# A two-part fp32 kernel on one core: the constant of a softmax sum added on another engine, an integer shift routed through PSUM, and a hand-planned list with new due steps

## The chip, the core and the metric

The kernel runs on one core of a Trainium2 chip. The metric is device time in microseconds (us) of one execution. The core has five engines that matter here: TensorE (PE, matmuls; PEld are its weight loads), VectorE (DVE), ScalarE (ACT), GpSimd (POOL) and SyncE (SP, which only issues DMAs). Each works through its own list of instructions in order and waits on semaphores for the others.

## The reference

An attention block and then a gated feed-forward block. The attention is computed per batch b (8) and head (8), with 512 tokens x and 32 state rows, head size 64:

```python
scores = scale * x @ state.T;  scores -= scores.max(-1)
a = exp(scores);   a /= a.sum(-1) + 1e-9;   xread = a @ state
scores2 = scale * state @ x.T; scores2 -= scores2.max(-1)
a2 = exp(scores2); a2 /= a2.sum(-1) + 1e-9; sread = a2 @ x
y = concat([xread, sread], axis=2)      # -> 4352 tokens x 512
h = y @ w_in        # 512 x 2048
g = h * cos(h)
out = g @ w_out     # 2048 x 512
```

x and state are float32; w_in and w_out arrive as float64 and are brought to float32 bits on the chip. "The constant" of the title is the 1e-9.

## The kernel before

**Data and stages.** Heads' reads are folded into the first feed-forward product: for each batch and each 512 columns of w_in, `products` (L484) multiplies the states with w_in, giving weight columns sw_all; a tile of h (128 hidden columns by 512 tokens) is then sw_all times the softmax weights aT_all. Each h tile goes through the gate: `gate` (L594, ACT: rounding to an integer, with bias 0.25), `gate2` (L601, DVE: subtract), `gate3` (L604, ACT: sine), `gate4` (L608, DVE: multiply, into g_all). The products of g with w_out collect in the two PSUM banks o (acc). From the third batch on, both products are done by a seven-product scheme on half-size blocks: `sw_sums` (L549, GpSimd) makes its weight sums, `seven_part` (L565, PE) its products, `seven_sum` (L583, DVE) the sums into h that the next part has to wait for, and `Product` does the same for w_out, with blocks fetched from DRAM into a ring and sums made on GpSimd.

**PSUM.** `at` has two banks (scores, transposes, reads), `o` two, and h_pairs[1] two, called side banks (L180, L181): in the first pair they hold the results of `products` until ACT or DVE has copied them to sw_all. Two more single banks hold the h tiles of the first pair, so the tile two places on waits for `gate4` of this one.

**An attention.** Class `Attention`: `max1` and `max2` reduce the scores, `spread1` spreads a row of 16 values per partition over a tile, `shift` subtracts, `exps` (L393, ACT) does both exponentials, the second one with its sums accumulated on the way into i12, `sums1` (L412, DVE) the sums of the first. `inverse` (L401) adds 1e-9 to the 34 sums per partition (32 of the first softmax, 2 of the second; the tile is named i_all in the profile) and takes the reciprocal, both on DVE; `spread1` and `norm1` (L422) then normalize. In the first pair `inverse1`, `inverse2` and `inverse12` call it, four times in all; later `spread2` (L415) calls it once for each of attentions 3 to 7.

**Conversion.** `fetch` (L226) loads a raw block of float64 pairs into slots of g_all, and `convert` (L238) makes float32 of it in five steps: "1" and "2" on ACT (magnitude of the high words, top bits of the low words), "b" on DVE (a shift left by 3, in place on SBUF), "c" on DVE (sign bit XORed in; one instruction with two tensors), "d" on GpSimd (an integer add). Blocks 0 to 3 have 512 elements per partition, blocks 4 to 17 have 1024. A block's slot comes free for the next raw block once "2" and "c" have read it.

**The order.** Two mechanisms set it. The first pair of batches (32 tiles, steps 0 to 31) is a hand-written list of tasks (`first_pair_tasks`, L1162). Each task has an engine, an assumed cost, the names of what it reads and writes, a due step, and a flag for those that need the port shared with GpSimd. `link` (L1559) derives the dependences and turns a due step into a time (22 + PACE x step), `first_pair` (L1595) then picks tasks engine by engine: among those that can start within NEAR of the earliest, the one due first. ARRIVED (L995) is when the first seven raw blocks are taken to be in; CONV and CONV_DUE (L1555, L1556) order the conversions of blocks 4 to 17; the raw load of a block is due three steps ahead of its conversion. Idle PE stretches at the start are filled with matmuls on zeros (`warm`). Instructions issued in this way carry line L44 in the profile.

Everything later is recorded on a tape (`taping[0]` is true) in program order, and `in_order` (L1821) reorders it by the assumed costs of `cost_of` (L1743) and by due times derived back from PE's place. `works_of` (L1773) marks the DVE operations taken to share the port with GpSimd. These instructions carry L1868. Nothing of either plan is decided at run time: each engine gets a fixed list.

Of the kernel before, what the change touches and what calls it, by code (L numbers as in the profile page):

```python
# [11 lines left out]
I32 = mybir.dt.int32  # L12
U32 = mybir.dt.uint32
ALU = mybir.AluOpType
# [8 lines left out]
def kernel(  # L23
# [32 lines left out]
    nc = Lanes  # L56
# [36 lines left out]
    TEMPS = 4  # L93
# [144 lines left out]
    def convert(i, p):  # L238
        if not f64:
            return  # L240
        raw, dst = raws[i], loads[i][0]
        bits = dst.bitcast(I32)
        m, w = dst.shape[1:]
        c0 = m * w if i in (2, 3) else 0
        e = low[i % 2][:, c0:c0 + m * w].rearrange("p (m f) -> p m f", m=m)
        e = e.bitcast(I32)
        if p == "1":
            nc.scalar.activation(dst, raw.bitcast(F32)[:, :, :, 1],
                                 func=ACTF.Abs, scale=2.0 ** -112)
        elif p == "2":  # L250
            nc.scalar.activation(e, raw.bitcast(U32)[:, :, :, 0],
                                 func=ACTF.Copy, scale=2.0 ** -29)
        elif p == "b":
            nc.vector.tensor_scalar(bits, bits, 3, None,
                                    op0=ALU.logical_shift_left)
        elif p == "c":
            nc.vector.scalar_tensor_tensor(out=bits, in0=raw[:, :, :, 1],
                                           scalar=-2 ** 31, in1=bits,
                                           op0=ALU.bitwise_and,
                                           op1=ALU.bitwise_xor)  # L260
        else:
            nc.gpsimd.tensor_tensor(bits, bits, e, op=ALU.add)
# [10 lines left out]
    class Attention:  # L273
# [126 lines left out]

        def inverse(self, v):  # L401
            w = v.rearrange("p (a b) -> p b a", b=2)
            nc.vector.tensor_scalar(w, w, 1e-9, None, op0=ALU.add)
            nc.vector.reciprocal(v, v)

        def inverse1(self):
# [585 lines left out]
                             stop=True)  # L992

    WARM, START_PE = 8, 19.7
    ARRIVED = (10.0, 11.3, 12.7, 14.0, 16.6, 19.3, 22.0)  # L995

    single_pool = singles.__enter__()
    for i in range(7 if f64 else 5):
# [163 lines left out]
    def first_pair_tasks():  # L1162
# [10 lines left out]
        def dve(n):  # L1173
            return .06 + n * .00108
# [23 lines left out]
        def conversion(i, due):  # L1198
            n = 512 if i < 4 else 1024
            raw, w, e = raw_of(i), weight_of(i), low_of(i)  # L1200
            if i > (6 if f64 else 4):
                add("sp", .4, lambda: fetch(i), "", raw, due - 3)
            for p, engine, cost, r, wr, sh in (
                    ("1", "act", act(n) + .05, raw, w, False),
                    ("2", "act", act(n) + .05, raw, e, False),
                    ("b", "dve", n * .0007 + .03, w, w, True),
                    ("c", "dve", dve(n), raw + " " + w, w, True),
                    ("d", "pool", pool(n), e + " " + w, w, False)):
                add(engine, cost, lambda p=p: convert(i, p), r, wr, due,
                    sh)  # L1210

        def attention(b, k):
# [26 lines left out]
            for j in range(2 if b == 0 else 0):  # L1239
                add("act", act(512) + .03,  # L1240
                    lambda j=j: a.exp1(slice(j, j + 1)), f"z{z}{j}",
                    f"z{z}{j}", k + 4)
            m2 = k + 6 if b == 0 else k + 4
            if b == 0:
                for j in range(2):
                    add("dve", .62, lambda j=j: a.sums1((j,)), f"z{z}{j}",
# [81 lines left out]
        def tile_(t, k):  # L1328
            n = t.b * NF + t.f
            h, z, c = n % 2, t.b % 2, t.f // 4 % 2  # L1330
            g = names(quads_of[t.row][t.i // QT], t.i % QT)
            add("pe", 1.72, lambda: hidden(t),
                f"sw{c}{t.f % 4 // 2}0 sw{c}{t.f % 4 // 2}1 z{z}0 z{z}1",
                f"h{h} H", k)
            add("act", act(512) - .04, lambda: gate(t), f"h{h}", f"q{h}")
            add("dve", dve(512) - .02, lambda: gate2(t), f"h{h} q{h}", f"q{h}")
            add("act", .63 if n else 1.91, lambda: gate3(t), f"q{h} T",
                f"q{h}")
            add("dve", dve(512) - .02, lambda: gate4(t), f"h{h} q{h}", g,
                k + 2)  # L1340

        def inner(which, m, q, temps, to, k, raw=True):
            for i in range(4):
# [144 lines left out]
            at_step[max(0, int(due) - 1)].append(  # L1488
                lambda i=i, due=due: conversion(i, due))
        for step, what in (  # L1490
                (1, lambda: attention_late(0, 0)),
                (3, lambda: products(0, 1, 2.5)),
                (3, lambda: add("pe", .4, lambda: states(1, side_banks[0]),
                                "held0", "sd00 sd01", 8.5)),
                (3, lambda: add("act", .53,
                                lambda: states_kept(1, side_banks[0]),
                                "sd00 sd01", "stT1", 5.5)),
                (5, lambda: attention(1, 4)),
                (7, lambda: products(0, 2, 4.5)),
                (11, lambda: products(0, 3, 11.5)),  # L1500
                (13, lambda: products(1, 0, 16)),
                (13, lambda: attention_late(1, 18)),
                (13, lambda: inner(0, a11, 5, temps[0], names(TEMPS), 14.5)),
                (15, lambda: sends(2, a22, 8, 17)),
                (15, lambda: sums_of(SQ, A21, A22, add_, 16, "pool")),
                (16, lambda: products(1, 1, 18.5)),
                (16, lambda: inner(3, matrix(SQ), SQ, temps[1], E, 17)),
                (17, lambda: sums_of(A22, SQ, A11, sub_, 16, "pool")),
                (17, lambda: attention(2, 19)),
                (18, lambda: sums_of(A21, A11, A21, sub_, 20, "dve")),  # L1510
                (20, lambda: products(1, 2, 23)),
                (20, lambda: inner(5, matrix(A21), A21, temps[0],
                                   names(TEMPS), 20)),
                (20, lambda: sends(1, a12, 6, 22)),
                (21, lambda: inner(4, matrix(A22), A22, temps[1], E, 22)),
                (23, lambda: sums_of(SQ, A12, A22, sub_, 23, "dve")),
                (24, lambda: inner(6, matrix(SQ), SQ, temps[0], names(TEMPS),
                                   25)),
                (24, lambda: products(1, 3, 31)),
                (25, lambda: attention_late(2, 25)),  # L1520
                (24, lambda: [add("sp", .4, lambda n=n: fetch_block(n), "B3",
                                  f"ring{n}", 27) for n in range(NB - 1)])):
            at_step[step].append(what)
        t32, t34 = all_tiles[PERIOD], all_tiles[PERIOD + 2]
        for step, what in (
                (26, lambda: outer(0, 2, 0, 0, 26, "dve")),
                (27, lambda: outer(0, 2, 0, 1, 27, "dve")),
                (28, lambda: tokens_of_next(32)),
                (28, lambda: products(2, 0, 28)),
                (28, lambda: p5_tasks(30.5)),  # L1530
                (29, lambda: weight_columns(t32, 30.5)),
                (29, lambda: add("dve", .7, lambda: halves(2, 0), "z00 z01",
                                 "E0", 30, True)),
                (29, lambda: add("dve", .7, lambda: halves(2, 1),
                                 "z00 z01 E0", "E1", 30, True)),
                (30, lambda: seven_tasks(t32, 29.5)),
                (31, lambda: weight_columns(t34, 32)),
                (32, lambda: outer(2, 3, 2, 0, 32, "dve")),
                (32, lambda: p3_sums(32))):
# [203 lines left out]
    def cost_of(engine, op, kw, aps):  # L1743
# [29 lines left out]
    def works_of(tape):  # L1773
        works, last, at_ = [], {}, 0.0
        wrote, read = {}, defaultdict(list)
        for engine, op, f, args, kw, n in tape:
# [167 lines left out]
```

## Time and profile before

| what | value |
|---|---|
| time, median of 3 runs | 739.65 us (737.28 to 739.89) |
| the profiled execution's own time | 744.15 us |
| its span, first to last instruction | 742.4 us |
| mean granted PE clock | 0.98 of full speed |
| instructions | 10,727 |
| first pair (L44), PE's last matmul ends | about 161 us |
| matmuls in the first pair's stretch 0 to 161 us, PE busy | 146.2 us |
| from 161 us on, PE busy | 558.5 of 581.4 us |

How to read it. The profile comes from one execution, which took 744.15 us by itself; its span leaves out 1.75 us around it. Busy time of PE is wall time with a matmul in flight, at whatever clock was granted. A row of the timeline gives start, duration, engine, line, operation, output<-inputs, and in square brackets how long the engine stood idle before it and what released it. For DVE and GpSimd the duration of a row includes any time that the instruction, already started, was held up. In the rows by tile, three numbers with slashes are shortest, median and longest duration in nanoseconds. In the list of waits, the numbers are the sum, the count and the longest.

### The profile page before, as it was taken

The page shows a single profiled execution, that of the slowest core. Times are in us where ns is not written, and L with a number is a line of the kernel's source. Part 1 is how long each engine was busy: PE and PEld are TensorE (multiplying, and loading weights), DVE is VectorE, ACT ScalarE, POOL GpSimd, SP SyncE. Part 2 cuts the span into 40 slices and gives each one's busy share as a digit, 9 for nine tenths or more (in the row PEclk, how much of TensorE's full clock was granted, in tenths as well). Part 3 has the DMA queues.
Part 4 walks back from the last instruction along what each step waited for, and adds up shares of the span by engine and source line. Part 5 has one row for each costly group of instructions (what it writes and reads, how often), then busy time and mean ns, then how long its engine had stood idle before and what let it go on. Part 6 is the DMA issues. An engine that isn't in the chain of part 4 may idle for free.

```text
span 742.4 us, 10727 instructions
## 1 busy us (share of the span) xinstructions
PE 704.7 (95%) x3628; PEld 525.4 (71%) x3628; DVE 524.7 (71%) x703; ACT 347.6 (47%) x586; POOL 536.9 (72%) x524
## 2 busy tenths in 40 slices
PE   8898799899959999999869999999999999999997
PEld 3343344477847878787757878887778888888886
DVE  4999769887897687788877667777875466725530
ACT  5788866654623446344624456343634443211110
POOL 1565779578974998988947975798978848896600
PEclk9999999999979999999979999999999999999999
DMA  9964689655517854783326734772356245455851
GB/s 299 291 223 154 214 229 326 137 144 139 143 42 141 218 131 119 154 182 82 97 54 133 183 79 103 154 177 79 107 135 178 86 100 130 113 195 175 220 104 29
DMA packets 204022, 111.34 MB, mean 150 GB/s; under 512 B 149888, under 2 KB 166784, under 8 KB 203968
## 3 DMA queue, kind: packets, MB, share of 16 engines
q1 hardware_dynamic: 202880, 110.14, 57.1%
q8 instruction: 29, 0.48, 0.3%
q10 hardware_dynamic: 960, 0.39, 0.2%
q14 instruction: 25, 0.20, 0.1%
q0 software_dynamic: 128, 0.13, 0.1%
HBM read 87.03 MB, written 23.59 MB: 149 GB/s over the span
## 4 chain that ended last, share of the span: by engine, by line
PE 79%; DVE 10%; ACT 5%; DMA 3%; issue 2%; SPq 1%; ACTq 0%; DVEq 0%
PE o L1868 39%; PE h L1868 22%; PE at L1868 8%; PE h L44 6%; PE o L44 4%; DVE i_all L1868 3%; DMA g_all<-in_moe_w_out_dram 2%; DVE g_all L44 2%; ACT q_all L44 1%; DVE q_all L44 1%; PE at L44 1%; ACT L44 1%; DVE q_all L1868 1%; DMA g_all<-blocks_kept 1%; DVE aS_all L1868 1%
## 5 line engine op out<-in xcount | busy, mean ns | idle before, releaser
L1868 POOL TENSOR_TENSOR g_all<-g_all 128x512 f32<-128x512 f32 x250 | 323.3, 1321 | 31.8 <-PE o L1868 21.3
L1868 PE MATMUL o<-g_all 128*128 128x256 f32 x1448 | 341.9, 382 | 0.0
L1868 PEld LDWEIGHTS o<-g_all 128*128 128x128 f32 x1448 | 273.7, 191 | 46.9 <-issue 5.6
L1868 ACT ACTIVATE q_all<-h 128x1024 int32<-128x1024 f32 (+1 forms) x56 | 54.0, 965 | 123.6 <-PE h L1868 122.1
L1868 DVE TENSOR_TENSOR q_all<-q_all,h 128x1024 f32<-128x1024 int32 (+1 forms) x56 | 63.9, 1141 | 48.1 <-ACT q_all L1868 47.8
L1868 DVE TENSOR_TENSOR g_all<-h,q_all 128x1024 f32<-128x1024 f32 (+1 forms) x56 | 64.0, 1142 | 25.7 <-ACT q_all L1868 23.6
L1868 PE MATMUL h<-aS_all,sw_all 128*128 128x256 f32 x188 | 57.4, 387 | 18.4 <-DVE h L1868 18.4
L1868 ACT ACTIVATE q_all<-q_all,halfpi 128x1024 f32<-128x1024 f32 (+1 forms) x56 | 61.1, 1091 | 27.5 <-DVE q_all L1868 27.2
L44 PE MATMUL h<-aT_all,sw_all 128*128 128x512 f32 (+1 forms) x132 | 65.5, 624 | 6.2 <-DVE g_all L44 6.2
L1868 DVE TENSOR_TENSOR h<-h,sums_all 128x256 f32<-128x256 f32 x94 | 40.2, 428 | 39.0 <-PE h L1868 33.7
L1868 DVE TENSOR_TENSOR g_all<-g_all 128x1024 f32<-128x1024 f32 (+1 forms) x68 | 67.5, 1036 | 0.1
L1868 POOL TENSOR_TENSOR swS_all<-sw_all 128x128 f32<-128x128 f32 x46 | 23.6, 514 | 49.3 <-ACT sw_all L1868 48.9
L1868 PE MATMUL h<-aS_all,swS_all 128*128 128x256 f32 x188 | 59.0, 396 | 0.0
L1868 PE MATMUL h<-aT_all,sw_all 128*128 128x256 f32 x188 | 56.6, 383 | 0.0
L1868 PEld LDWEIGHTS h<-aS_all,sw_all 128*128 128x128 f32 x188 | 35.6, 192 | 25.0 <-DVE h L1868 10.1
L44 PEld LDWEIGHTS h<-aT_all,sw_all 128*128 128x128 f32 x132 | 24.5, 197 | 37.5 <-issue 20.5
L1868 PEld LDWEIGHTS h<-aS_all,swS_all 128*128 128x128 f32 x188 | 34.0, 191 | 21.3 <-POOL g_all L1868 10.1
L44 POOL TENSOR_TENSOR g_all<-g_all 128x512 f32<-128x512 f32 x30 | 40.4, 1363 | 7.4 <-DVE g_all L44 4.8
L44 PE MATMUL o<-g_all 128*128 128x512 f32 (+1 forms) x112 | 43.7, 520 | 0.0
L44 POOL TENSOR_TENSOR w_in<-w_in,aS_all 128x1024 int32<-128x1024 int32 (+1 forms) x10 | 21.4, 2155 | 27.8 <-DVE w_in L44 22.5
L1868 POOL TENSOR_TENSOR held<-held 128x512 f32<-128x512 f32 x16 | 21.2, 1329 | 26.3 <-DVE held L1868 22.2
L1868 PEld LDWEIGHTS h<-aT_all,sw_all 128*128 128x128 f32 x188 | 35.8, 192 | 5.5 <-DVE g_all L1868 0.6
(159 smaller groups left out, 983.0 us busy)
## 6 DMA issues: line engine op xcount, KB each, us to landing
g_all<-blocks_kept SPq DMA_DIRECT2D x206, 256.0 KB, 2.8
blocks_kept<-g_all SPq DMA_DIRECT2D x48, 256.0 KB, 4.0
g_all<-in_moe_w_out_dram SPq DMA_DIRECT2D x8, 1024.0 KB, 5.7
out_dram<-ot SPq DMA_DIRECT2D x128, 64.0 KB, 2.8
g_all<-in_moe_w_in_dram SPq DMA_DIRECT2D x6, 1024.0 KB, 7.2
x_b<-in_x_dram SPq DMA_DIRECT2D x24, 256.0 KB, 4.7
xT<-in_x_dram SPq DMA_DIRECT2D x80, 64.0 KB, 2.9
x_b<-in_x_dram SPq DMA_DIRECT2D x16, 128.0 KB, 4.1
```

Of the source, the lines that this page charges most:

```text
L44: return f(*args, **kw)
L1868: f(*args, **kw)
```

## The change

Three things change.

1. `inverse`, while the tape is recorded (attentions 3 to 7), adds 1e-9 with one ACT instruction; the reciprocal stays on DVE. The four calls of the first pair keep the add on DVE. `cost_of` gives an ACT instruction at least 0.19, and `works_of` no longer counts a DVE tensor_scalar among the operations that share the port.
2. Step "b" of blocks 4 to 17 writes the shifted words to the two side banks in PSUM, and "c" reads them there and writes the result to SBUF. In the list, "b" costs as an ordinary DVE operation, and for these blocks "b" and "c" don't have the flag for the shared port; they name the side banks sd00 to sd11 as written and read, so they stand in order with `products`. Blocks 0 to 3 keep the shift in place.
3. ARRIVED, CONV, CONV_DUE, PACE (3.4 to 3.6), NEAR (0.3 to 0.1) and most due steps of the list are set to other values.

The core of the diff:

```diff
+        shifted = bits if i < 4 else h_pairs[1].bitcast(I32)
...
-            nc.vector.tensor_scalar(bits, bits, 3, None,
+            nc.vector.tensor_scalar(shifted, bits, 3, None,
                                     op0=ALU.logical_shift_left)
...
-                                           scalar=-2 ** 31, in1=bits,
+                                           scalar=-2 ** 31, in1=shifted,
...
         def inverse(self, v):
             w = v.rearrange("p (a b) -> p b a", b=2)
-            nc.vector.tensor_scalar(w, w, 1e-9, None, op0=ALU.add)
+            if taping[0]:
+                nc.scalar.activation(v, v, func=ACTF.Copy, bias=1e-9)
+            else:
+                nc.vector.tensor_scalar(w, w, 1e-9, None, op0=ALU.add)
             nc.vector.reciprocal(v, v)
...
-    ARRIVED = (10.0, 11.3, 12.7, 14.0, 16.6, 19.3, 22.0)
+    ARRIVED = (10.7, 12.1, 13.5, 14.8, 18.2, 20.9, 23.9)
...
+            x, narrow = (w, True) if i < 4 else ("sd00 sd01 sd10 sd11", False)
+            b_cost = n * .0007 + .03 if narrow else dve(n)
...
-                    ("b", "dve", n * .0007 + .03, w, w, True),
-                    ("c", "dve", dve(n), raw + " " + w, w, True),
+                    ("b", "dve", b_cost, w, x, narrow),
+                    ("c", "dve", dve(n), raw + " " + x, w, narrow),
...
-            m2 = k + 6 if b == 0 else k + 4
+            m2 = k + 6 if b == 0 else k + 1.0
...
             add("dve", dve(512) - .02, lambda: gate4(t), f"h{h} q{h}", g,
-                k + 2)
+                k + 7.5)
...
-                (1, lambda: attention_late(0, 0)),
-                (3, lambda: products(0, 1, 2.5)),
+                (1, lambda: attention_late(0, 3.0)),
+                (3, lambda: products(0, 1, 14.0)),
...
-                first(step - 4, step - 1)
+                first(step - 4, step + 13)
...
-                    second(i, step)
+                    second(i, step + 23.0)
...
-    CONV = (4, 5, 6, 7, 8, 9, 10, 11, 14, 15, 16, 17, 12, 13)
-    CONV_DUE = (3, 4.5, 3.5, 6, 6.7, 8.5, 9, 9.5, 12.0, 11, 11.3, 13.7, 12.5, 15.7)
-    PACE, NEAR, SEND = 3.4, 0.3, 2.5
+    CONV = (4, 5, 6, 7, 8, 9, 11, 10, 14, 15, 16, 17, 12, 13)
+    CONV_DUE = (1.8, 1.5, 2.1, 5.2, 5.3, 5.2, 10.8, 9.3, 9.7, 11.1, 12.6, 13.2, 13.1, 15.7)
+    PACE, NEAR, SEND = 3.6, 0.1, 2.5
...
-            return (.1 if n > S else .08) + n * .00099
+            return max(.19, (.1 if n > S else .08) + n * .00099)
...
             if engine == "dve" and op in ("tensor_tensor",
-                                          "scalar_tensor_tensor",
-                                          "tensor_scalar"):
+                                          "scalar_tensor_tensor"):
```

More of the change, by code (lines that the diff above doesn't have):

```diff
@@ L1490, in first_pair_tasks @@
         for step, what in (
-                (1, lambda: attention_late(0, 0)),
-                (3, lambda: products(0, 1, 2.5)),
+                (1, lambda: attention_late(0, 3.0)),
+                (3, lambda: products(0, 1, 14.0)),
                 (3, lambda: add("pe", .4, lambda: states(1, side_banks[0]),
-                                "held0", "sd00 sd01", 8.5)),
+                                "held0", "sd00 sd01", 13.5)),
                 (3, lambda: add("act", .53,
                                 lambda: states_kept(1, side_banks[0]),
-                                "sd00 sd01", "stT1", 5.5)),
@@ L1498, in first_pair_tasks @@
[L1498 to L1503, printed above, removed]
-                (15, lambda: sends(2, a22, 8, 17)),
-                (15, lambda: sums_of(SQ, A21, A22, add_, 16, "pool")),
-                (16, lambda: products(1, 1, 18.5)),
@@ L1507, in first_pair_tasks @@
[L1507 to L1511, printed above, removed]
+                                "sd00 sd01", "stT1", 14.5)),
+                (5, lambda: attention(1, 3.5)),
+                (7, lambda: products(0, 2, 11.0)),
+                (11, lambda: products(0, 3, 13.0)),
@@ new lines, in first_pair_tasks @@
+                (13, lambda: products(1, 0, 12.0)),
+                (13, lambda: attention_late(1, 26.5)),
+                (13, lambda: inner(0, a11, 5, temps[0], names(TEMPS), 8.0)),
+                (15, lambda: sends(2, a22, 8, 17)),
+                (15, lambda: sums_of(SQ, A21, A22, add_, 22.5, "pool")),
+                (16, lambda: products(1, 1, 29.5)),
+                (16, lambda: inner(3, matrix(SQ), SQ, temps[1], E, 29.0)),
+                (17, lambda: sums_of(A22, SQ, A11, sub_, 35.5, "pool")),
@@ L1512, in first_pair_tasks @@
+                (17, lambda: attention(2, 27.5)),
+                (18, lambda: sums_of(A21, A11, A21, sub_, 38.5, "dve")),
+                (20, lambda: products(1, 2, 14.5)),
                 (20, lambda: inner(5, matrix(A21), A21, temps[0],
-                                   names(TEMPS), 20)),
+                                   names(TEMPS), 24.5)),
                 (20, lambda: sends(1, a12, 6, 22)),
-                (21, lambda: inner(4, matrix(A22), A22, temps[1], E, 22)),
-                (23, lambda: sums_of(SQ, A12, A22, sub_, 23, "dve")),
+                (21, lambda: inner(4, matrix(A22), A22, temps[1], E, 17.0)),
@@ L1517, in first_pair_tasks @@
+                (23, lambda: sums_of(SQ, A12, A22, sub_, 19.5, "dve")),
                 (24, lambda: inner(6, matrix(SQ), SQ, temps[0], names(TEMPS),
                                    25)),
-                (24, lambda: products(1, 3, 31)),
-                (25, lambda: attention_late(2, 25)),
+                (24, lambda: products(1, 3, 28.0)),
+                (25, lambda: attention_late(2, 36.0)),
                 (24, lambda: [add("sp", .4, lambda n=n: fetch_block(n), "B3",
@@ L1525, in first_pair_tasks @@
         for step, what in (
[L1526 to L1531, printed above, removed]
+                (26, lambda: outer(0, 2, 0, 0, 19.5, "dve")),
+                (27, lambda: outer(0, 2, 0, 1, 24.0, "dve")),
+                (28, lambda: tokens_of_next(23.5)),
+                (28, lambda: products(2, 0, 19.5)),
+                (28, lambda: p5_tasks(29.5)),
+                (29, lambda: weight_columns(t32, 22.5)),
                 (29, lambda: add("dve", .7, lambda: halves(2, 0), "z00 z01",
@@ L1535, in first_pair_tasks @@
                                  "z00 z01 E0", "E1", 30, True)),
-                (30, lambda: seven_tasks(t32, 29.5)),
+                (30, lambda: seven_tasks(t32, 27.5)),
                 (31, lambda: weight_columns(t34, 32)),
```

## The prediction

> **What bounds the kernel now.** I read the page first: shares, slices, chain. Then TensorE's waits, the timeline around the longest ones, and the instructions on the tile of sums, i_all.
>
> ```profile
> PE 704.7 (95%) x3628; PEld 525.4 (71%) x3628; DVE 524.7 (71%) x703; ACT 347.6 (47%) x586; POOL 536.9 (72%) x524
> PE   8898799899959999999869999999999999999997
> PE 79%; DVE 10%; ACT 5%; DMA 3%; issue 2%; SPq 1%; ACTq 0%; DVEq 0%
> ```
>
> TensorE is the bound: busy 95%, 79% of the chain. So a microsecond is won where PE stands still or runs at a lower clock, and nowhere else. The slices (18.6 us each) show where: the first nine (the hand-planned first pair, L44, up to 161 us), and two single dips, the 5 in slice 12 and the 6 in slice 21. The waits of PE name who ends them:
>
> ```profile
> PE h L1868 <- DVE h L1868: 18.4, 5, 8.7
> PE h L44 <- DVE g_all L44: 6.2, 8, 1.9
> PE at L44 <- ACT xT L44: 4.5, 3, 2.4
> ```
>
> In the recorded part (L1868) PE waits only 18.4 us, and two of the five waits (8.7 and 7.8 us) are nearly all of it: the two dips. The timeline of VectorE, GpSimd and PE there:
>
> ```profile
> 202.92 11.59 DVE L1868 TENSOR_SCALAR i_all<-i_all 128x34 f32<-128x34 f32 x1
> 214.54 0.37 DVE L1868 RECIPROCAL i_all<-i_all 128x34 f32<-128x34 f32 x1
> ...
> 214.01 0.46 POOL L1868 TENSOR_TENSOR swS_all<-swS_all,sw_all 128x128 f32<-128x128 f32 x1
> 218.46 2.18 POOL L1868 TENSOR_TENSOR held<-held 128x512 f32<-128x512 f32 x1 [3.99 <-PE h L1868]
> ...
> 365.54 9.32 DVE L1868 TENSOR_SCALAR i_all<-i_all 128x34 f32<-128x34 f32 x1
> ```
>
> The add of 1e-9 to 34 sums stands 11.59 us on VectorE. It ends when GpSimd's run of back-to-back instructions ends (214.01 + 0.46). Behind it in VectorE's queue is the sum into h that PE waits for. The five adds of this part:
>
> ```profile
> L1868 DVE TENSOR_SCALAR i_all<-i_all x5: 186/761/11593, 202.9 to 527.2; 128x34 f32<-128x34 f32 x5
> L1868 DVE TENSOR_TENSOR g_all<-g_all x68: 277/1216/2336, 166.2 to 710.8; 128x1024 f32<-128x1024 f32 x36, 128x128 f32<-128x128 f32 x32
> ```
>
> An undisturbed add takes 0.19 us; two of five starve. Two-input operations on SBUF (second line) meet the same GpSimd runs and were never held longer than 2.34 - 1.21 = 1.1 us, less than one GpSimd instruction of 1.27.
>
> **What the Trainium skill says.** "SBUF — State Buffer", Who interferes with whom: VectorE in a two-port mode, which tensor_scalar can enter, and GpSimd exclude each other from a shared port pair, and the one that issues first keeps it for its whole instruction. The trace agrees that they exclude each other; a wait over fourteen GpSimd instructions is more than the page states. "VectorE: DVE Perf Modes", Why PSUM operands drop a tier: an fp32 operation with a PSUM operand runs at one element a cycle; the trace of before has no shift into PSUM. "TensorE: Matmul & The Clock Gate", What's actually happening: after idling, matmuls run at half clock for a while; the trace agrees: four matmul passes (L44, 67.38) took 3.68 us after a gap, 1.88 otherwise. "ScalarE: Activation LUTs", What ACT_TABLE_LOAD costs, prices an ACTIVATE with immediate bias at 186 ns + 0.833 ns per element: an estimated 0.21 us for 34; the trace has 0.19 for 128x2 (m_all).
>
> **The change, part by part.**
>
> *The add on ScalarE, five attentions.* First stall: PE falls idle at 207.73 (matmuls at 205.84, 1.89 long) and the pair at 225.63 starts 17.9 us later. Between them lie 6.9 us of matmuls at the duration they have elsewhere (two seven-product parts 0.43 + 0.86, another 0.86, two stages of 1.73, the reads 1.02, 0.3 of gaps). Excess 11.0: 8.65 wait, 2.35 lower clock. Second: 369.23 to 382.76 = 13.5, of which 3.65 is work; excess 9.85. Together 20.9 us. For what is late next, the other three attentions serve: their adds took 0.29, 0.19 and 0.76, and PE was 99 to 100% busy around them (99.3 of 100 us in 400:500 and in 500:600). GpSimd's backlog isn't next: after the first stall it idles 4 us, then 6.1 and 4.9 more in the next 20 (busy 3.9 and 5.1 of 10), so the 8.65 us fit.
>
> The new wait: add on ACT, then reciprocal on DVE. In the built order the add stands behind the copies of sw_all on ACT, which before ended at 202.7 in the first case, and DVE has the reciprocal behind gate2 and one sum, at about 202.9: the hand-over waits for nothing. But reciprocal and spread (0.37 + 1.25) now come ahead of the first sum into h, which then ends at 204.95, while PE wants it at 204.1: 0.85 us lost. Bounds per attention: 0 and 1 (the sum's cover is one stage of 1.73). I take 1.5 us for five. The normalization that follows can be held 1.1 us; it is needed tiles later. On ACT 5 x 0.2 us lie in 47% idle time. Net 19.4.
>
> *The shift through PSUM.* Fourteen shifts of 1024 elements took 8.0 + 6.2 = 14.2 us, mean 1.02, shortest 0.69, longest 2.52: the excess over 0.69 is waiting for GpSimd. Through PSUM one costs between 0.69 (if the fast mode held) and 1.22 (a 1024 operation with a PSUM input); the page says the latter, I take 1.17: VectorE gains no time (16.4 against 14.2), but neither side waits for the other; GpSimd's fourteen adds (36.2 us) could shrink to 14 x 2.36 = 33.0. The price is the side banks: products of weight columns must wait for the XOR before, and the next shift for ACT's copies (0.5 each).
>
> *Arrival times and due steps.* They change only the order in the first pair. PE's multiset, SP's 548 rows and the count of warm-up matmuls stay. I followed the built order by hand: each instruction starts at the end of the one ahead on its engine or when its releaser is done, with durations from the rows of before (gate 0.5, gates 2 and 4 0.6, sine 0.62, raw conversion 1.05 to 1.1, XOR 1.15, GpSimd adds 2.4, tile on PE 1.72). Raw block 9 now goes ahead of 7 and 8 on SP (1 MB each; 5.7 to 7.2 to land); ACT reaches none before it lands. The next attention's tokens are asked for after the reads (84.6) and land about 91 to 93, when PE turns to them. The hand-followed starts of tiles on PE, before / after: tile 0 25.2 / 26.7 (the two maxima now stand behind the shifts, so the second softmax is late); tile 4 41.3 / 43.7; tile 9 67.4 / 68.3; tile 12 82.2 / 78.7; tile 16 96.7 / 91.2 with one product less done; tile 23 122.2 / 120.5 with 1.9 us more products done; tile 27 140.7 / 131.1 with two products (3.45) less done. The part ends at 161.0 / 155.3: 5.6 us. What goes are waits of 1.9, 1.0, 1.0, 1.2 and 1.1 between 65 and 92 us, and the ones around 131 to 136; in their place are 0.6, 1.6, 1.7 and 1.4. One slowed group (1.8) must be added, since the gap of 1.6 is like the one at 65.3. Net gain 4, bounds -3 (a loss: each of the last three gaps slowed, and 2 us of DMA lateness) and 10 (nearly all of PE's 11 us of waits after 20 us).
>
> *Sum.* 19.4 + 4 = 23.4. The profiled execution took 744.15 us, of which 742.4 span: 720.7 for its like. The three timed runs stand 4.5 us lower at the median; if the stalls were absent there they would stand 20 lower. So 739.65 - 23.4 = 716.2.
>
> **Rivals.**
> 1. Forecast, 716.2: 62%.
> 2. The stalls go, but the first pair gains nothing or loses up to 3, since DVE is 86% busy from 20 to 161 us and the new order has early tiles later: 739.65 - 19.4 + 1 = 721. For: tiles 0 to 9 are behind. Against: the walk gains later. 20%.
> 3. Half of the starving returns at the next user of the shared port (the normalization, or ACT's copies waiting for GpSimd's sums in front of the add): 739.65 - 10 - 4 = 726. For: same GpSimd runs. Against: the second line on i_all's port above, 1.1 us at most. 11%.
> 4. The timed executions have shorter stalls than the profiled one, or the change doesn't reach them: within 0.5%. 3%.
> 5. Slower: three adds stay on VectorE, in the first pair. The third was asked at 128.59, just as a GpSimd run that began at 102.6 ended, and took 0.43. If the new order brings it to the head of such a run, VectorE stands for its 26.4 us, with 2.3 of lower clock behind: 739.65 - 23.4 + 28 = 744. It decides only if that wait passes 23.4 us on PE. Against: in the new order these GpSimd instructions carry waits for DMAs, and the add comes near 120. 4%.
>
> **From these to the numbers.** Low end: 20.9 whole and 9.7 in the first pair, 709. High end: rival 3 and a little, 727. Faster by over 0.5% (about what a measurement of this kernel can tell from no change): 62 + 20 + 11, 93%; within 3%; slower 4%.
>
> **What would show it.** In the new profile: no VectorE operation on i_all above 2 us after 161; PE's wait for DVE h below 5 us in total; slices 12 and 21 at 9; five ACT operations on i_all of about 0.2; shifts into h of 1.15 to 1.2; PE's last L44 matmul near 155 to 158. Wrong if PE's waits for DVE h stay above 10 us, or if the L44 part ends after 161.

## The result and the profile after

The changed kernel takes 730.5 us at the median of four runs (728.7 to 732.09). The kernel before, on the same chip, takes 739.77 us (737.28 to 743.71). The ratio is 0.9869, 95% interval [0.982, 0.9919]: 9.3 us gained where 23.4 were forecast. The profiled execution took 730.02 us with a span of 728.2, against 744.15 and 742.4 before. Ratios here and below are of executions within 1.5% of the fastest of their kernel in the same comparison; medians and ranges are of all executions except one of before at 1039 us and the profiled one of e12 at 1862 us, so e12 has no profile here.

The same three lines of the page as before the change: busy time by engine, PE's slices (18.2 us each now), the chain that ended last by engine.

```profile
PE 702.1 (96%) x3628; PEld 524.2 (72%) x3628; DVE 511.6 (70%) x698; ACT 348.6 (48%) x591; POOL 533.1 (73%) x524
PE   8899799999969999999999999999999999999997
PE 83%; DVE 8%; ACT 3%; issue 2%; DMA 2%; SPq 1%; DVEq 0%; ACTq 0%
```

Of the two dips in PE's row the later one is gone; the earlier one, a 6 in slice 12, is still there. PE's waits (in all, how many, the longest):

```profile
PE h L1873 <- DVE h L1873: 8.3, 4, 6.8
PE h L44 <- DVE g_all L44: 6.6, 6, 1.4
PE at L44 <- ACT xT L44: 2.6, 2, 2.1
```

In the recorded part (L1873 now) one wait of 6.8 us is left of the 8.7 and 7.8. The timeline around it shows who makes it (start, duration; in brackets the idle time before and its releaser):

```profile
199.12 0.35 DVE L1873 RECIPROCAL i_all<-i_all 128x34 f32<-128x34 f32 x1
...
201.47 10.07 DVE L1873 TENSOR_TENSOR aT_all<-aT_all,xT 128x1024 f32<-128x1024 f32 x1
211.47 1.21 DVE L1873 TENSOR_TENSOR g_all<-h,q_all 128x1024 f32<-128x1024 f32 x1
212.60 0.41 DVE L1873 TENSOR_TENSOR h<-h,sums_all 128x256 f32<-128x256 f32 x1
...
201.02 2.50 POOL L1873 TENSOR_TENSOR g_all<-g_all 128x512 f32<-128x512 f32 x2
...
210.00 0.46 POOL L1873 TENSOR_TENSOR swS_all<-swS_all,sw_all 128x128 f32<-128x128 f32 x1
214.01 1.26 POOL L1873 TENSOR_TENSOR held<-held 128x512 f32<-128x512 f32 x1 [3.56 <-DVE held L1873]
...
213.07 1.22 PE L1873 MATMUL h<-aS_all,sw_all 128*128 128x256 f32 x2 [6.78 <-DVE h L1873]
```

The add isn't on VectorE any more, and the reciprocal runs at 199.12 undisturbed. Now the normalization (aT_all<-aT_all,xT, two inputs from SBUF) stands 10.07 us where it took 1.20 before. Its own work comes only after GpSimd's run of back-to-back instructions has ended (210.00 + 0.46 = 210.46; the normalization ends 1.08 us later), as with the add. Below, an instruction held in this way over several GpSimd instructions is called starved. Two instructions behind it in VectorE's queue is the sum into h that PE wants. The loss is more than the wait of 6.78 us, because PE also runs slower behind it: the first two matmuls take 1.22 us where such a pair takes 0.59, and from 200 to 230 us the granted clock is 0.83. This is attention 3, the first of the recorded part.

In attention 5, where the second add of before had starved, the normalization came in the middle of such a run too, and got in after one GpSimd instruction. VectorE and GpSimd there:

```profile
367.77 2.20 DVE L1873 TENSOR_TENSOR aT_all<-aT_all,xT 128x1024 f32<-128x1024 f32 x1
...
367.61 3.50 POOL L1873 TENSOR_TENSOR g_all<-g_all 128x512 f32<-128x512 f32 x2
```

GpSimd's two instructions took 3.50 us in place of 2.50: one of them was held while the normalization went through.

### The profile page after: what moved, and what is told of

Same layout as the page of the kernel before. It is cut to its first block, busy times and chain, and to the rows that moved or that the text cites. A ratio compares the mean times of both kernels' runs of the same rounds, so it can differ in the third digit from the quotient of the medians.

```text
span 728.2 us, 10719 instructions
## 1 busy us (share of the span) xinstructions
PE 702.1 (96%) x3628; PEld 524.2 (72%) x3628; DVE 511.6 (70%) x698; ACT 348.6 (48%) x591; POOL 533.1 (73%) x524
## 4 chain that ended last, share of the span: by engine, by line
PE 83%; DVE 8%; ACT 3%; issue 2%; DMA 2%; SPq 1%; DVEq 0%; ACTq 0%
PE o L1873 42%; PE h L1873 23%; PE at L1873 8%; PE h L44 5%; PE o L44 3%; DVE g_all L44 1%; PE at L44 1%; ACT q_all L44 1%; DMA x_b<-in_x_dram 1%; DVE g_all L1873 1%; SPq L44 1%; DVE w_in L44 1%; DVE h L44 1%; DVE q_all L44 1%; ACT aS_all L44 1%
## 5 line engine op out<-in xcount | busy, mean ns | idle before, releaser
L1873 POOL TENSOR_TENSOR g_all<-g_all 128x512 f32<-128x512 f32 x250 | 329.1, 1344 | 37.9 <-PE o L1873 22.2
L1873 PE MATMUL o<-g_all 128*128 128x256 f32 x1448 | 341.7, 382 | 0.0
L1873 PEld LDWEIGHTS o<-g_all 128*128 128x128 f32 x1448 | 273.6, 191 | 47.3 <-issue 6.2
L1873 ACT ACTIVATE q_all<-h 128x1024 int32<-128x1024 f32 (+1 forms) x56 | 54.1, 966 | 108.6 <-PE h L1873 107.2
L1873 DVE TENSOR_TENSOR q_all<-q_all,h 128x1024 f32<-128x1024 int32 (+1 forms) x56 | 64.0, 1142 | 57.0 <-ACT q_all L1873 56.9
L1873 DVE TENSOR_TENSOR g_all<-h,q_all 128x1024 f32<-128x1024 f32 (+1 forms) x56 | 64.1, 1144 | 24.2 <-ACT q_all L1873 22.5
L1873 ACT ACTIVATE q_all<-q_all,halfpi 128x1024 f32<-128x1024 f32 (+1 forms) x56 | 61.1, 1091 | 24.4 <-DVE q_all L1873 24.0
L1873 DVE TENSOR_TENSOR h<-h,sums_all 128x256 f32<-128x256 f32 x94 | 40.2, 427 | 38.7 <-PE h L1873 33.7
L1873 DVE TENSOR_TENSOR g_all<-g_all 128x1024 f32<-128x1024 f32 (+1 forms) x68 | 67.1, 1026 | 0.1
L1873 PE MATMUL h<-aS_all,sw_all 128*128 128x256 f32 x188 | 56.8, 384 | 8.3 <-DVE h L1873 8.3
L1873 PE MATMUL h<-aS_all,swS_all 128*128 128x256 f32 x188 | 58.9, 395 | 0.0
L1873 PE MATMUL h<-aT_all,sw_all 128*128 128x256 f32 x188 | 56.6, 383 | 0.0
L1873 POOL TENSOR_TENSOR swS_all<-sw_all 128x128 f32<-128x128 f32 x46 | 23.3, 506 | 40.1 <-ACT sw_all L1873 39.7
L1873 PEld LDWEIGHTS h<-aS_all,swS_all 128*128 128x128 f32 x188 | 34.0, 191 | 20.5 <-POOL g_all L1873 7.5
L44 POOL TENSOR_TENSOR g_all<-g_all 128x512 f32<-128x512 f32 x30 | 40.6, 1375 | 11.2 <-DVE g_all L44 9.4
L1873 PEld LDWEIGHTS h<-aS_all,sw_all 128*128 128x128 f32 x188 | 35.6, 191 | 14.5 <-DVE h L1873 9.3
L44 POOL TENSOR_TENSOR w_in<-w_in,aS_all 128x1024 int32<-128x1024 int32 (+1 forms) x10 | 19.6, 1963 | 33.2 <-DVE w_in L44 32.3
L1873 PEld LDWEIGHTS h<-aT_all,sw_all 128*128 128x128 f32 x188 | 35.8, 192 | 5.5 <-DVE g_all L1873 0.6
L1873 DVE SCALAR_TENSOR_TENSOR held<-o,held 128x512 f32<-128x512 f32 x38 | 26.1, 686 | 13.9 <-PE o L1873 13.3
```

The costliest lines, as they stand in the source:

```text
L44: return f(*args, **kw)
L1873: f(*args, **kw)
```

## The experiments

Each edit is to the changed kernel unless a line says that it starts from before. Kernels between two rules of the table ran on one chip and share the runs of before, whose median stands with the first of them.

| kernel | median us (range) | ratio to before [95%] |
|---|---|---|
| e1_add_alone (before 742.92) | 727.46 (725.55 to 732.02) | 0.9805 [0.9775, 0.9835] |
| e2_first_alone | 724.90 (719.06 to 736.58) | 0.9729 [0.9688, 0.9770] |
| e3_norm_gpsimd | 725.13 (722.40 to 726.95) | 0.9768 [0.9739, 0.9798] |
| e4_gpsimd_waits | 719.94 (719.61 to 722.26) | 0.9703 [0.9677, 0.9729] |
| --- | | |
| e5_old_pair_waits (before 741.64) | 720.34 (718.80 to 722.43) | 0.9757 [0.9700, 0.9813] |
| e6_dve_add_waits | 720.37 (719.03 to 721.22) | 0.9750 [0.9699, 0.9800] |
| e7_copy_no_wait | 725.06 (720.89 to 733.53) | 0.9802 [0.9742, 0.9861] |
| e8_shift_in_place | 727.97 (726.89 to 735.35) | 0.9869 [0.9810, 0.9928] |
| --- | | |
| e9_before_waits (before 743.43) | 719.61 (716.34 to 721.89) | 0.9696 [0.9656, 0.9737] |
| e10_old_steps_psum | 733.98 (732.52 to 740.00) | 0.9892 [0.9858, 0.9927] |
| e11_changed_again | 731.64 (728.91 to 736.72) | 0.9867 [0.9820, 0.9914] |
| e12_waits_again | 721.83 (719.72 to 722.55) | 0.9724 [0.9685, 0.9764] |
| --- | | |
| e13_two_input_no_wait (before 739.62) | 721.46 (720.67 to 728.73) | 0.9796 [0.9742, 0.9849] |
| e14_copy_no_wait_again | 722.08 (721.38 to 729.84) | 0.9822 [0.9760, 0.9885] |
| e15_one_stop | 722.12 (720.18 to 726.68) | 0.9792 [0.9742, 0.9842] |

### Each part of the change alone

e1_add_alone starts from before and takes only the add on ACT, with its list price:

```
+            if taping[0]:
+                nc.scalar.activation(v, v, func=ACTF.Copy, bias=1e-9)
```

> Theory (the gain is the second starved add of before; the first one's starving has only passed to the normalization): the add on ACT alone gives nearly the whole gain, 728 to 731 us, and attention 3's normalization takes about 10 us again; should the normalization ask at a moment when it gets in, 720 to 723. Rival (the gain comes from the first pair's new order): 736 us or more.

Measured 727.5 us, half a microsecond under the theory's range. The normalization of attention 3 takes 7.10 us (at 204.44); six GpSimd instructions ended before it got in.

e2_first_alone is the changed kernel with the add back on DVE:

```
-            if taping[0]:
-                nc.scalar.activation(v, v, func=ACTF.Copy, bias=1e-9)
```

> The changed kernel with the add back on DVE in the recorded part, its price there as before. Theory: the first pair alone is worth the 1.6 us by which its end moved in the trace, so 737 to 740 us, with one or two adds above 5 us in attentions 3 and 5. Rival (the first pair carries the gain): 733 us or less.

My theory missed here: 724.9 us, and no add above 1.25 us in the profile. By the letter the rival (the first pair carries the gain) has it. But each half of the change then looks faster alone than both halves together (ratios 0.9805 and 0.9729 against 0.9869; the interval of e1 just overlaps that of the changed kernel, that of e2 does not), so neither theory holds as put: the parts don't add up. What marks e2 is its spread: four runs from 719.1 to 727.0 us, two at 734.6 and 736.6. Its profile, of a run of 722.8 us, has a normalization of 5.01 us at 357.14 and a difference into aS_all of 3.25 us at 212.03, so the starving has changed its victim. That the two long runs are starving too isn't shown, since neither was profiled; e7 and e14 below, one kernel profiled twice, show that it can differ from one execution to the next.

### Taking the starving away

e3_norm_gpsimd puts the normalization of the recorded part on GpSimd, so that it can no longer hold up VectorE's queue:

```
-            nc.vector.tensor_tensor(self.aT[:, js], self.z1[:, js],
-                                    self.spread[:, js], op=ALU.mult)
+            engine = nc.gpsimd if taping[0] else nc.vector
+            engine.tensor_tensor(self.aT[:, js], self.z1[:, js],
+                                 self.spread[:, js], op=ALU.mult)
```

> The changed kernel with the normalization of the recorded part on GpSimd, an estimated 2.4 us each there. Theory (PE's 6.8 us gap is the sum into h queued behind a starved normalization): no DVE instruction above 3 us between 190 and 215 us, the gap and the 2.5 us at lower clock behind it go, 720 to 724 us. Rival (GpSimd's backlog itself is what PE waits for): GpSimd has 12 us more to do, 730 us or more.

Measured 725.1 us, 1 us outside the theory's range and well below the rival's. The five normalizations take 2.35 to 2.39 us each on GpSimd. No VectorE instruction is above 3 us between 190 and 215 us. PE's waits for h fall from 8.3 to 2.4 us in all. The next victim shows as well: aS_all<-aT_all takes 3.70 us at 367.46.

e4_gpsimd_waits leaves the normalization on VectorE and adds a GpSimd instruction that waits for it:

```
             nc.vector.tensor_tensor(self.aT[:, js], self.z1[:, js],
                                     self.spread[:, js], op=ALU.mult)
+            if taping[0]:
+                nc.gpsimd.tensor_copy(mark, self.aT[:, 1, 0:8])
```

> The changed kernel and, in each recorded attention, one tiny GpSimd copy that reads the normalization's output, so that GpSimd's run has to stop for it; nothing taken out. Theory (DVE gets in where GpSimd's queue stops): attention 3's normalization falls from 10.07 us to between 1.4 and 3.7 us, PE's gap of 6.8 us to under 1.5 us, 720 to 724 us. Rival (GpSimd's backlog is what PE waits for): the copy's wait delays GpSimd by 1.2 us more, 730 to 733 us.

Measured 719.9 us, and 721.8 on another chip (e12). PE's and ACT's orders are those of the changed kernel to the last instruction; VectorE's differs in a few places long after attention 3. The timeline of e4 at the same place:

```profile
201.65 3.15 DVE L1876 TENSOR_TENSOR aT_all<-aT_all,xT 128x1024 f32<-128x1024 f32 x1
204.73 1.21 DVE L1876 TENSOR_TENSOR g_all<-h,q_all 128x1024 f32<-128x1024 f32 x1
205.86 0.42 DVE L1876 TENSOR_TENSOR h<-h,sums_all 128x256 f32<-128x256 f32 x1
...
201.21 2.51 POOL L1876 TENSOR_TENSOR g_all<-g_all 128x512 f32<-128x512 f32 x2
204.87 0.19 POOL L1876 COPY mark<-aT_all 128x8 f32<-128x8 f32 x1 [1.14 <-DVE aT_all L1876]
```

After the pair of GpSimd instructions the copy stands still for 1.14 us, the normalization goes through, and the sum into h starts at 205.86 in place of 212.60. From 200 to 230 us PE is now busy 29.84 us at a granted clock of 1.00, against 23.22 us at 0.83 in the changed kernel. GpSimd's backlog is not what PE waited for: GpSimd was delayed, and the time fell.

> e4_gpsimd_waits again, on the same chip as the three others: 719 to 722.5 us, all runs within 4 us, and 8 to 11 us below the changed kernel.

> The changed kernel itself, five rounds more and a second profile. Theory (attention 3's normalization is starved in most executions): 727 to 733 us, a normalization above 6 us near 201 us in this profile too. Rival (its 10 us in the first profile was a single bad execution): runs below 722 us among these.

Both came as expected, but for one run of e11 at 736.7. Side by side the changed kernel takes 731.6 us and the one with the five copies 721.8: 9.8 us apart. Attention 3's normalization takes 10.08 us in e11's profile (10.07 in the first one), so this starving is no accident of one execution.

### How much is that one instruction?

e15_one_stop has the copy of e4 in attention 3 only:

```
+            if taping[0] and self.b == 3:
+                nc.gpsimd.tensor_copy(mark, self.aT[:, 1, 0:8])
```

> The changed kernel with a single instruction more: the tiny GpSimd copy that waits for the normalization, in attention 3 only. Theory (of the 14 us that the forecast missed, 10 are this one starved instruction): normalization about 3.2 us, 720 to 723 us. Rival (the gain of the five copies comes from other places): 727 us or more.

Measured 722.1 us. PE, VectorE, ACT and SP have exactly the changed kernel's order and GpSimd has one instruction more, so nothing else in the lists has moved:

```profile
203.04 3.12 DVE L1876 TENSOR_TENSOR aT_all<-aT_all,xT 128x1024 f32<-128x1024 f32 x1
...
207.21 0.42 DVE L1876 TENSOR_TENSOR h<-h,sums_all 128x256 f32<-128x256 f32 x1
...
206.22 0.19 POOL L1876 COPY mark<-aT_all 128x8 f32<-128x8 f32 x1 [1.15 <-DVE aT_all L1876]
```

The normalization is down from 10.07 to 3.12 us, and most of the 9.8 us is gone: 730.5 and 731.6 without the copy, on other chips. By the ratios to before (0.9792 against 0.9869) it would be 5.6 us; but the runs of before spread from 730.1 to 743.4 us on this chip, so that ratio says less than e12's. Its runs reach 726.7, though, and its profile has the next victim, aS_all<-aT_all, with 3.45 us at 213.52 (1.40 in e4).

### What is the change worth without the starving?

e5_old_pair_waits has the first pair of before and e4's recorded part (e1 and the copy). e6_dve_add_waits is e4 with the add on DVE and a second copy that waits for the add. e9_before_waits starts from before, takes nothing of the change itself, and has the two copies. In the recorded part the new instructions also make `in_order` place about two dozen of VectorE's 703 instructions, as many of GpSimd's, and a few of ACT's elsewhere in their lists; the first pair's lists stay as they were:

```
             nc.vector.tensor_scalar(w, w, 1e-9, None, op0=ALU.add)
+            if taping[0]:
+                nc.gpsimd.tensor_copy(mark, v[:, 0:8])
             nc.vector.reciprocal(v, v)
```

> The first pair of the kernel before, with the recorded part of e4_gpsimd_waits: the add on ACT and GpSimd's copy that waits for the normalization. With the starving out of both, the distance to e4 (719.9 us) is what the first pair's new order is worth. Forecast's step (4 us gained): 723 to 725 us. Theory from the end of the first pair in e1 (157.1 us against 159.6 to 159.7 in after and e4): the new order gains nothing or loses up to 2.5 us, 717 to 720.5 us.

> The changed kernel with the add back on DVE, and two tiny GpSimd copies in each recorded attention, one that waits for the add and one that waits for the normalization. Theory (the move to ACT is worth only the chance of starving that it takes away): as e4, 719 to 722 us, with all runs within 4 us where the same kernel without the copies had runs from 719 to 737. Rival (the ACT add has a worth of its own): 724 us or more with narrow runs.

> The kernel before with nothing of the change, and in each recorded attention two tiny GpSimd copies, one that waits for the add on DVE and one for the normalization. Theory (the whole gain of the change, and the part of the forecast that it missed, is starving that such a stop removes): 719 to 723 us, with all runs within 4 us. Rival (the add's move to ACT or the first pair's order has a worth of its own): 725 us or more.

All three theories held, except that e9's runs spread over 5.6 us where 4 were expected. With the stops in (the copies that wait), the medians of the four combinations lie within 0.8 us:

| with the stops | first pair of before | first pair changed |
|---|---|---|
| add on DVE | 719.61 (e9) | 720.37 (e6) |
| add on ACT | 720.34 (e5) | 719.94 (e4) |

These are three chips. On one chip e5 and e6 are equal, and e9 lies 2.2 us below e12 (721.83, the kernel of e4), with overlapping runs. So neither the move to ACT nor the new first pair has a worth of its own that shows here. Ten tiny copies make the kernel before 24 us faster than it was (719.6 against 743.4), and 12 us faster than the changed one on the same chip (731.6). Part of these 24 us could be the new order of the lists rather than the stops; no run separates the two for e9, as e15 does for the changed kernel. In e9's profile, the adds and normalizations (count, shortest / median / longest in ns), PE's slices, and its wait for h:

```profile
L1873 DVE TENSOR_SCALAR i_all<-i_all x5: 178/405/1816, 202.3 to 504.2; 128x34 f32<-128x34 f32 x5
L1873 DVE TENSOR_TENSOR aT_all<-aT_all,xT x5: 1202/1214/1365, 208.8 to 510.0; 128x1024 f32<-128x1024 f32 x5
```

```profile
PE   8898889999999999999999999999999999999997
```

```profile
PE h L1873 <- DVE h L1873: 0.7, 1, 0.7
```

The longest add is 1.8 us where it was 11.6, and the row has no dip after the first pair.

### The two halves of the first pair's change

e8_shift_in_place is e4 with the shift back in place and its old list price; e10_old_steps_psum is e5 with the shift through PSUM under the old steps:

```
-        shifted = bits if i < 4 else h_pairs[1].bitcast(I32)
+        shifted = bits
```

> e4_gpsimd_waits with the shift back in place in SBUF (its list price with it) and everything else of the first pair as changed. Forecast's step (the shift through PSUM brings DVE no gain: 1.22 us each measured against 1.0 in place): 717 to 720.5 us. Rival (in place a shift holds GpSimd and is held by it, which the changed due steps don't allow for): 722 us or more.

> e5_old_pair_waits (720.3 us) with one thing of the first pair's change added: the conversion's shift through PSUM with its list prices, under the old arrival times and due steps. Forecast's step (the shift through PSUM brings DVE no gain and costs it 0.2 us each): 719.5 to 722 us. Rival (shift and due steps belong together, as e8's 728.0 us suggests): 723 us or more.

Both rivals were right. With the shift in place under the new steps 728.0 us, 8 more than e5 and e6 on the same chip; with the shift through PSUM under the old steps 734.0, 14 more than e9 on the same chip. PE's last matmul of the part then ends at 167.1 and 173.4 us, against 159.7 in e4. In e10's profile, PE's waits in the first pair:

```profile
PE h L44 <- DVE g_all L44: 11.3, 8, 4.4
```

PE waits 11.3 us for VectorE's g_all (5.4 in e5), though the shifts are as long as in e4 (1.22 us). In e8 the fourteen shifts even take less of VectorE than in e4 (8.6 + 4.1 us against 9.8 + 7.3). So it is not VectorE's time for them that costs; GpSimd's fourteen adds take 2.7 us more (35.8 against 33.1). In both kernels the shift's price, its names and its flag change with it, and the list comes out in another order. Shift and due steps belong together in this sense: under the old steps the shift through PSUM, with the order that follows from it, loses 12 us against e12 and 14 against e9 on the same chip, and the new steps win them back. Which part of that order costs is open.

### What lets VectorE in

e7_copy_no_wait and e14_copy_no_wait_again have e4's copies in e4's places, reading a constant tile, so that GpSimd waits for nothing; e13_two_input_no_wait has a tiny sum of two inputs there:

```
+            if taping[0]:
+                tape.append(("pool", "tensor_copy",
+                             lambda *_: tc.nc.gpsimd.tensor_copy(mark, idle),
+                             (mark, self.aT[:, 1, 0:8]), {}, burst[0]))
```

> e4_gpsimd_waits with its copies in the same places of GpSimd's queue, reading a constant tile, so that GpSimd waits for nothing there. Theory (DVE gets in because GpSimd's queue stops): nothing of the 10 us is given back, 728 to 732 us as the changed kernel, attention 3's normalization 5 us or longer. Rival (any small instruction between the long ones, or the shift in time that it makes, lets DVE in): 719 to 723 us.

> e7_copy_no_wait again. Theory (a copy that waits for nothing lets the normalization in but leaves other DVE instructions to be starved): normalization of attention 3 about 3.2 us again, runs from 720 to 735 us, spread over more than 5 us.

> e7_copy_no_wait with each tiny copy replaced by a tiny sum of two inputs from SBUF, of the same size, in the same places, waiting for nothing. Theory A (in e7 it was the copy's kind, one input, that let DVE in): attention 3's normalization above 8 us again, 728 to 733 us. Theory B (any instruction more, or the shift in time that it makes, changes who wins): 3 to 4 us, and runs spread over more than 4 us as e7's.

My theory for e7 (it takes a stop) fell. In e7's profile:

```profile
201.03 3.16 DVE L1880 TENSOR_TENSOR aT_all<-aT_all,xT 128x1024 f32<-128x1024 f32 x1
...
347.17 5.83 DVE L1880 TENSOR_TENSOR g_all<-g_all 128x1024 f32<-128x1024 f32 x1
...
203.03 1.21 POOL L434 COPY mark<-idle 128x8 f32<-128x8 f32 x1
```

The copy waits for no semaphore, yet the normalization gets in ahead of it (the copy takes 1.21 us in place of 0.19). But a g_all<-g_all starves 5.83 us at 347.17, another 5.82 us at 506.59, and this execution took 733.5 us. That execution was the slowest of e7's six. In the profile of e14, the same kernel, neither of the two is starved in a run of 721.6 us; the first of them there:

```profile
347.69 2.14 DVE L1880 TENSOR_TENSOR g_all<-g_all 128x1024 f32<-128x1024 f32 x1
```

e14's normalization takes 3.12 us, and its runs spread again (721.4 to 729.8); e13 gives 3.15 us and 720.7 to 728.7. The kind of the tiny instruction made no difference here (theory B of e13), and a further instruction in that place was enough for the one victim. Within 4 us over all runs stay only kernels where GpSimd has to wait for the normalization in every attention (e4, e5, e6, e12), if the changed kernel's ten runs are taken together (728.7 to 736.7). That isn't sufficient: e9 spreads over 5.6 us, none of it above 722, and e8 and e10, which have the stops as well, over 8.5 and 7.5 us, with one long run each that was not profiled.

## Why the prediction was right and wrong

**Right: what held PE, and what the add cost.** The two stalls were priced at 20.9 us; e9, with the stops and the list order that they bring, gains 24. The second stall went as forecast: PE is busy 30.00 of 30 us from 360 to 390, against 22.22 before. There was luck in that: the normalization of attention 5 asked inside a GpSimd run too, and why it was held only 1.0 us there and 8.9 in attention 3 the runs don't say. The five adds on ACT take 0.235 to 0.267 us (0.21 estimated), and PE's list of waits has none for them.

**The step that failed: the normalization "can be held 1.1 us; it is needed tiles later".** The bound came from two-input operations on SBUF that had not been held longer in the one profile of before, 36 large ones and 32 small ones of g_all. I took this for a difference in kind between them and the add. It is none: the runs have the normalization at 10.07 us and a g_all<-g_all at 5.83. That nothing of the sort was in one profile was chance or place, and the runs don't tell which. With the add gone the normalization comes 2.35 us after the reciprocal (201.47 less 199.12) into the same GpSimd run, and is held until its end. And while its own reader may be tiles away, in VectorE's queue the sum into h that PE needs stands two places behind it. Rival 3 had this mechanism, at 726 us, and I gave it 11%. "SBUF — State Buffer" of the Trainium skill, Who interferes with whom, says that a VectorE instruction with two SBUF inputs contends with a GpSimd instruction that reads SBUF, and that the order of issue, not the operation's shape, decides who blocks. The measured 10.07 us on a two-input operation agree with the first statement, and I had cited the section for tensor_scalar alone. They don't agree with the order of issue: by the profile ten GpSimd instructions that began after the normalization (201.47) went ahead of it.

**The second term mis-sized: the first pair's net gain of 4.** The hand-followed part ends at 155.3; in the profile it ends at 159.6 (155.93 + 3.62). The tiles' starts slid: tile 12 at 79.9 for 78.7, tile 23 at 123.8 for 120.5. PE's waits for VectorE's g_all in this part still add up to as much (6.2 us before, 6.6 after). And what it was measured against moves too: the old order's part ends at 161.1 in before, 160.5 in e9, 157.1 in e1 and 155.8 in e5, at granted clocks of 0.91, 0.96, 1.00 and 1.00 between 60 and 100 us. The new order's part ends between 159.1 and 161.6 in its ten profiles. By the runs the gain is none (table above), which is rival 2's first pair. My bounds of -3 and 10 held it. Why the walk came out 4 us early is not traced further.

**The sum with these two.** 716.2, plus 9.8 for the starved normalization (e11 less e12), plus 4: 730.0, measured 730.5. Its two terms come from other chips than its base, so this agreement is no proof.

**Misread, without weight in the sum.** ACT's 47% is its busy share, not idle time. The first pair keeps four adds on VectorE, not three; the one at 128.59 is the fourth. The 82.2 given for tile 12 before is about the start of tile 13 (tile 12: 80.5), and the 0.69 called the shortest shift is about the median (shortest 0.64).

**Right, in the small.** Shifts into PSUM: 1.221 and 1.220 us each, 17.1 in all (1.17 and 16.4 forecast; I had shaded the 1.22 that the bound said). GpSimd's fourteen adds: 18.9 + 14.2 = 33.1 us, 33.0 forecast. Those two lines of the changed kernel's first pair, grouped by form (busy us, mean ns):

```profile
L44 DVE TENSOR_SCALAR h<-g_all 128x1024 int32<-128x1024 int32 x8 | 9.8, 1221 | 0.7 <-ACT g_all L44 0.6
L44 DVE TENSOR_SCALAR h<-w_in 128x1024 int32<-128x1024 int32 x6 | 7.3, 1220 | 0.1
```

**The signs.** No VectorE operation on i_all above 2 us, five ACT operations, slice 21 at 9: as said. PE's wait for h below 5 us, slice 12 at 9, the part's end by 158: not so. The slower rival had no place: the first pair's adds took 0.41 us at most.

## What to carry to other kernels

When an instruction is seen starved by another engine, ask which of its neighbours in the queue could be held by the same engine: taking away the victim can hand its place to the next of them, and whoever is queued behind that one then waits nearly as long. A bound read from instructions that happened not to meet the bad moment is no bound; look for what would have to be different for them to meet it. And when two halves of a change are each faster alone than together, or one kernel's runs spread over 17 us, suspect a race between engines, remove it in all versions alike (here by an instruction that makes the long run stop), and compare them then. If the schedule is rebuilt from the new instructions, compare the lists as well: a stop that changes nothing else (e15) proves more than one that also reorders (e9).

## What the hardware did that I had not expected

- Not the add alone was starved over several GpSimd instructions in a row, but VectorE's operations with two inputs from SBUF too: aT_all 10.07, 7.10 and 5.01 us, g_all 5.83, aS_all 3.2 to 3.7, where they take 1.2, 1.2 and 0.4 undisturbed. It is rare: in sixteen profiles more than 700 such operations and adds of the recorded part were held by 0.1 us or more, and 15 of them were passed by at three or more ends of GpSimd instructions.
- A single GpSimd instruction of 0.19 us, in a place where it does nothing for the result, takes 8 to 9 us off the kernel (e15, medians across chips; 5.6 by the ratios).
- What decides who wins at the end of a GpSimd instruction is open. The g_all<-g_all at 347.17 in e7 began 3.91 us after the start of a run of eight equal GpSimd instructions, and starved. In e14, the same kernel, the same instruction began 3.92 us after the start of the same run, and was held 0.94 us (so was the one in e4, at 346.60). The same instructions in the same order thus ended either way, and I tried nothing finer.
